# A fused attention and MLP block: the second LayerNorm's factors of twelve tiles stored a chunk ahead, the MLP's last block evacuated at once, three buffers of normalised rows in the front

## The chip, the cores and the metric

The kernel runs on one core of a Trainium2 chip. The metric is the device time of one execution in microseconds (us), the median of several. The core has five engines that work side by side, each through its own list of instructions in the order in which they were written: TensorE (PE, matrix products, transposes, with its weight loads shown as PEld), VectorE (DVE), ScalarE (ACT), GpSimd (POOL) and SyncE (SP), which here only issues DMAs. An engine waits at an instruction until what it needs has been produced by the others, and everything behind that instruction on the same engine waits with it.

## What is computed

The input x has 2048 rows of 448 values. The reference, cut to what matters:

```python
xn = _layernorm(x)
out = x + A(xn, wq, wk, wv, wo) + B(xn, w1, b1, w2, b2)

# A: 16 heads of 28, one shared key and value head
q = (x @ wq).reshape(B, S, H, Dh); k = x @ wk; v = x @ wv
p = softmax(einsum("bhqd,bkd->bhqk", q, k) * Dh ** -0.5)
o = einsum("bhqk,bkd->bhqd", p, v) @ wo

# B: pre-LayerNorm, 448 -> 1792 -> 448
y = _layernorm(x)
h = gelu(einsum("bsd,df->bsf", y, w1) + b1)
o = einsum("bsf,fd->bsd", h, w2) + b2
```

The MLP normalises rows that are normalised already. Their mean is zero, so the second LayerNorm is one factor for each row, worked out from the first one's variance and reciprocal deviation. The kernel multiplies the product with w1 by that factor.

## The kernel before

Products are taken to fp32 accuracy by splitting each operand into a high and a low part (names ending in h and l) and adding three products: high by low, high by high, low by high. The 2048 rows are 16 tiles of 128, in four chunks of four tiles (512 rows). Three stages follow each other on PE.

**Front: normalising and projecting, to about 64 us.** For each chunk c, `q_slot(c, i)` with i = 0 to 3 (L349) makes one quarter of the query, key and value columns: eleven matmuls on PE into a PSUM bank `qp`. The pieces around them are written slot by slot in the loop at L429. After slot (c, i) stand the evacuation of the slot before (`evac`, L357: ACT copies the high part to `qe`, DVE subtracts to get the low part, SP stores both to DRAM in `qd`; for i = 0 also the key `ks`, `kl` and the value `vt`, which PE turns in `v_slot`), then the parts of the next chunk's preparation, then w1's or w2's splitting, then further jobs from a table (`later`, L402). The preparation of a chunk (`norm_parts`, L258) has two parts for each tile k. *Centre* (`c`): ACT writes the normalised rows to a buffer `xn` (L271), DVE the last 64 columns again (L272, called the tail in what follows). *Turn* (`t`): four PE transposes into a PSUM buffer `m` (L280), ACT copies the high part `xh` (L281), DVE subtracts the low part `xl` (L282). There are three PSUM buffers `m`, in turn, and two buffers `xn`. The statistics are DVE's `bn` (L207, one per tile) and `bn_end` (L211 and the reciprocal chain of `rstd`, L189).

**The second LayerNorm's factors.** `norm_both` (L228) makes the factors of all 16 tiles in three steps, after slots (2,2), (2,3) and (3,0): products and first step of the reciprocal chain on DVE, the rest of the chain, then a PE transpose (L237), DVE's copy to `rows` (L239) and SP's store to `second` in DRAM (L240). `load_factors` (L248) reads 512 of them back, spread over all 128 partitions, into an `xn` buffer; it stands after slots (3,1) and (3,2) for the first two chunks of the MLP, which takes the chunks in the order 2, 3, 0, 1.

**MLP, to about 354 us.** There are 56 blocks, n = 14c + ft: a chunk by 128 of the 1792 hidden columns. Slot n runs `mlp1` of block n (L585: eleven first-layer matmuls into `ph`, for the blocks 1 to 3 into an `m` buffer; DVE multiplies by the factors at L592 into `hx`; ACT squares it into `hz` and adds the bias; *inner*, DVE L599; *middle*, tanh on ACT L602 and DVE L603; *ending*, ACT L609 copies `hh`, DVE L610 subtracts `hl`) and `mlp2` of block n − 3 (L614: twelve matmuls of 448 columns with `w2h`, `w2l` at L621, L624 and L627 into four PSUM banks `m2`). Middle and ending of a block are written one slot later, behind the next block's multiply (L592 to L594). w2 is split in the first chunk's slots (ACT L340, DVE L343); `w2h` and `w2l` take the storage that the front's buffers, `qe` among them, had before. With a chunk's last block DVE adds the four `m2` banks to the rows `a` (L631). In the last four blocks of chunk 3 (n = 52 to 55) a few jobs of the attention's start are written between matmuls: `first_shift` (DVE L533), `first_exp` (ACT L536), `first_back` (DVE L542), and one early score each.

**Attention and output, to the end.** Scores on PE (L681), exponents on ACT (L682), products with the values on PE (L870), then the output projection. Scores take the PSUM storage of `m2` once the MLP is over.

Of the kernel before, what the change touches and what calls it, by code (L numbers as in the profile page):

```python
# [40 lines left out]
def block_kernel(ctx, tc, x, wq, wk, wv, wo, w1, b1, w2, b2, out):  # L41
# [4 lines left out]
    def f(t):  # L46
        return t.bitcast(F32)
# [23 lines left out]
    lnq = wp.tile([P, NT], F32, name="lnq")  # L71
# [156 lines left out]
    def norm_both():  # L228
        dve.tensor_mul(lnq, lnp[:, :, 1], lnr)
        dve.tensor_mul(lnq, lnq, lnr)  # L230
        r = rstd(lnq, lnq, NT)
        next(r)
        yield
        next(r)
        yield
        turned = mtile([NT, P])
        pe.transpose(turned, lnq, ident)  # L237
        rows = wp.tile([NT, P], F32, name="rows")
        dve.tensor_copy(rows, turned)  # L239
        nc.sync.dma_start(second, rows)  # L240
        act.activation(warm, one, AF.Tanh)
        yield
# [5 lines left out]
    def load_factors(c):  # L248
        factors[c] = tmp.tile([P, CW], F32, name="xn", bufs=2)
        nc.sync.dma_start(factors[c], second[CT * c:CT * c + CT, :].rearrange("k p -> (k p)")[None, :].to_broadcast([P, CW]))  # L250
# [7 lines left out]
    def norm_parts(c, first=False, bank=mtile):  # L258
# [3 lines left out]
        xns = {}  # L262

        def center(k):
            t = CT * c + k
            if first:
                xn = f(wqp.tile([P, 2, CW], F32R, name="qe", bufs=5))[:, 0, :]
            else:
                xn = tmp.tile([P, 4 * P], F32, name="xn", bufs=2)
            scale, bias, src = lnr, lnb, xin[t]  # L270
            act.activation(xn[:, 0:D], src, AF.Identity, bias=bias[:, t:t + 1], scale=scale[:, t:t + 1])  # L271
            dve.tensor_scalar(xn[:, D:512], src[:, 384:448], scale[:, t:t + 1], bias[:, t:t + 1],  # L272
                              op0=ALU.mult, op1=ALU.add)
            xns[k] = xn

        def turn(k):
            sl = slice(k * P, (k + 1) * P)
            pt = bank([P, 4, P])
            for b in range(4):
                pe.transpose(pt[:, b, :], xns[k][:, b * P:(b + 1) * P], ident)  # L280
            act.activation(xh[:, :, sl], pt, AF.Copy)  # L281
            dve.tensor_sub(xl[:, :, sl], pt, f(xh[:, :, sl]))  # L282

        return center, turn

    def norm_first(bank):
        center, turn = norm_parts(0, True, bank)
# [117 lines left out]
    for c, at in ((2, ((0, 1), (0, 2), (0, 2), (0, 3))), (3, ((1, 0), (1, 1), (1, 2), (1, 3)))):  # L405
# [5 lines left out]
    g = norm_both()  # L411
    for c, k in ((2, 2), (2, 3), (3, 0)):
        later(c, k, lambda g=g: next(g))
# [15 lines left out]
    for c in range(NCH):  # L429
        if c + 1 < NCH:  # L430
            center, turn = norm_parts(c + 1)
        for i in range(4):
# [9 lines left out]
            for part, k in (("", "c0 c1", "t0 c2 t1 c3", "t2 t3") if c == 0 else  # L442
                            ("c0 c1", "t0 c2 t1 c3", "t2 t3", ""))[i].split() if c + 1 < NCH else ():
                (center if part == "c" else turn)(int(k))
# [5 lines left out]
            if (c, i) in ((3, 1), (3, 2)):  # L450
                load_factors(MLP_ORDER[i - 1])
# [133 lines left out]
    def mlp1(c, ft, before):  # L585
# [6 lines left out]
        dve.tensor_mul(hx, ph, factors[MLP_ORDER[c]])  # L592
        for job in before:
            job()  # L594
# [41 lines left out]
    def slot(n):  # L636
# [383 lines left out]
```

## Time and profile before

| | us |
|---|---|
| median of 3 runs | 905.06 (904.57 to 905.09) |
| the profiled execution | 903.79 |
| its span in the trace | 902.0 |
| PE busy in it | 886.1 (98%) |
| ACT busy | 703.6 (78%) |
| DVE busy | 488.4 (54%) |
| POOL busy | 68.6 (8%) |

The profiled execution is one of its own, so its time differs a little from the median, and what lies outside its span is 1.8 us. PE's mean granted clock is 0.995 of full speed. The page cuts the span into 40 slices of 22.55 us:

```profile
PE   9998999999999999999999999999999999999997
PEclk9998999999999999999999999999999999999999
```

Each digit is the busy share, or for PEclk the granted clock, in tenths. Both show 9 (90% or more) nearly throughout. The fourth slice (67.7 to 90.2 us) holds the start of the MLP; there both rows show an 8. The last holds the end of PE's work.

### The profile page before, as it was taken

How to read it: one execution, taken by the hardware profiler on the slowest of the kernel's cores; microseconds unless marked ns; L12 is line 12 of the kernel's file. 1: busy time of each engine (PE TensorE's matmuls, PEld its weight loads, DVE VectorE, ACT ScalarE, POOL GpSimd, SP SyncE). 2: the span in 40 equal slices, each digit the busy share in tenths (PEclk: the TensorE clock that was granted, in tenths of full speed). 3: DMA queues.
4: the chain of work that ended last, by engine and by line, in shares of the span. 5: the costliest groups of instructions: out<-in, count | busy, mean ns of one | idle time of the engine just before them, and what ended most of it. 6: DMA issues, size and time to landing. Idle time of an engine off the chain costs nothing.

```text
span 902.0 us, 13217 instructions
## 1 busy us (share of the span) xinstructions
PE 886.1 (98%) x4914; PEld 566.0 (63%) x4914; DVE 488.4 (54%) x975; ACT 703.6 (78%) x1334; POOL 68.6 (8%) x70
## 2 busy tenths in 40 slices
PE   9998999999999999999999999999999999999997
PEld 8776888888888886444444564444564444564445
DVE  6855676556556776654564544554544554544212
ACT  5765565555545456999999969999969999969992
POOL 4350000000000002031000000000000000000000
PEclk9998999999999999999999999999999999999999
DMA  9994133004002013031102211002211002211001
GB/s 290 323 285 138 42 114 125 10 20 162 6 1 77 6 42 115 9 78 43 22 21 57 70 41 43 18 25 55 70 41 43 22 22 55 71 41 41 3 1 44
DMA packets 36297, 60.69 MB, mean 67 GB/s; under 512 B 7782, under 2 KB 23348, under 8 KB 35204
## 3 DMA queue, kind: packets, MB, share of 16 engines
q1 hardware_dynamic: 34820, 59.22, 21.6%
q8 instruction: 40, 0.66, 0.3%
q10 hardware_dynamic: 1408, 0.57, 0.2%
q14 instruction: 29, 0.24, 0.1%
HBM read 39.89 MB, written 18.88 MB: 65 GB/s over the span
## 4 chain that ended last, share of the span: by engine, by line
PE 87%; ACT 5%; DVE 4%; DMA 3%; issue 1%; SPq 0%; ACTq 0%; DVEq 0%
PE m L681 26%; PE po L870 25%; PE ph L177 11%; PE m L627 5%; PE m L624 5%; PE m L621 4%; ACT p L682 2%; PE m L521 2%; PE m L757 1%; PE m L758 1%; PE m L759 1%; PE ph L180 1%; PE ph L182 1%; PE qp L177 1%; DMA second<-rows 1%
## 5 line engine op out<-in xcount | busy, mean ns | idle before, releaser
L682 ACT ACTIVATE p<-m 128x512 f32<-128x512 f32 x956 | 490.1, 758 | 30.2 <-PE m L681 29.7
L681 PE MATMUL m<-xh,ks 128*128 128x512 f32 x960 | 272.6, 410 | 0.6 <-DVE tt L528 0.3
L681 PEld LDWEIGHTS m<-xh,ks 128*128 128x128 f32 x960 | 174.3, 188 | 149.4 <-ACT p L682 76.3
L870 PE MATMUL po<-p,vs 128*32 128x512 f32 x2016 | 242.4, 598 | 0.0
L595 ACT ACTIVATE hz<-hx,b1s 128x512 f32<-128x512 f32 x56 | 40.6, 726 | 112.8 <-DVE hx L592 112.8
L870 PEld LDWEIGHTS po<-p,vs 128*32 128x32 f32 x2016 | 52.6, 109 | 115.8 <-issue 115.8
L528 DVE STREAM_TRANSPOSE tt<-m 128x512 f32<-128x512 f32 x60 | 43.0, 716 | 110.6 <-PE m L521 110.6
L621 PE MATMUL m<-w2h,hh 128*128 128x448 f32 x224 | 83.1, 371 | 5.1 <-ACT w2h L340 3.8
L624 PE MATMUL m<-w2l,hh 128*128 128x448 f32 x224 | 82.8, 370 | 0.4 <-DVE w2l L343 0.4
L627 PE MATMUL m<-w2h,hl 128*128 128x448 f32 x224 | 82.8, 370 | 0.2
L599 DVE SCALAR_TENSOR_TENSOR hz<-hz,hx 128x512 f32<-128x512 f32 x56 | 38.8, 692 | 53.7 <-ACT hx L596 53.7
L797 DVE COPY oc<-po 128x512 f32<-128x512 f32 x15 | 10.4, 692 | 103.2 <-PE po L870 103.2
L177 PE MATMUL ph<-xh,w1h 128*128 128x512 f32 x159 | 62.9, 396 | 0.1
L592 DVE TENSOR_TENSOR hx<-ph,xn 128x512 f32<-128x512 f32 x53 | 36.5, 690 | 48.5 <-PE ph L182 42.6
L177 PE MATMUL ph<-xh,w1l 128*128 128x512 f32 x159 | 62.3, 392 | 0.0
L177 PE MATMUL ph<-xl,w1h 128*128 128x512 f32 x159 | 62.3, 392 | 0.0
L812 POOL TENSOR_TENSOR otl<-oc,oth 128x512 fp32r<-128x512 f32 x15 | 23.9, 1591 | 470.4 <-DVE oth L810 274.1
L536 ACT ACTIVATE tt<-tt 128x512 f32<-128x512 f32 x60 | 50.0, 834 | 0.0
L621 PEld LDWEIGHTS m<-w2h,hh 128*128 128x128 f32 x224 | 42.6, 190 | 11.2 <-ACT w2h L340 4.3
L542 DVE STREAM_TRANSPOSE p<-tt 128x512 f32<-128x512 f32 x60 | 42.1, 702 | 12.0 <-ACT tt L536 12.0
L624 PEld LDWEIGHTS m<-w2l,hh 128*128 128x128 f32 x224 | 42.6, 190 | 5.4 <-DVE w2l L343 0.8
L627 PEld LDWEIGHTS m<-w2h,hl 128*128 128x128 f32 x224 | 42.6, 190 | 4.4 <-DVE hl L610 0.9
(174 smaller groups left out, 1033.1 us busy)
## 6 DMA issues: line engine op xcount, KB each, us to landing
xh<-qd SPq DMA_DIRECT2D x64, 224.0 KB
qd<-qe SPq DMA_DIRECT2D x24, 256.0 KB
a<-in_A_x_dram SPq DMA_DIRECT2D x20, 224.0 KB
ad<-a SPq DMA_DIRECT2D x16, 224.0 KB
a<-ad SPq DMA_DIRECT2D x16, 224.0 KB
raw<-in_B_w_dram SPq DMA_DIRECT2D x7, 448.0 KB
out_dram<-a SPq DMA_DIRECT2D x14, 224.0 KB
xd<-xh SPq DMA_DIRECT2D x2, 1024.0 KB
```

Source lines behind the costliest of these rows:

```text
L177: pe.matmul(ps, w, v, start=(n == 0), stop=False)
L528: dve.transpose(tts[u, j], pm)
L536: act.activation(tts[u, j], tts[u, j], AF.Exp, scale=SCALE)
L542: dve.transpose(p0s[u][:, j], tts.pop((u, j)))
L595: act.activation(hz, hx, AF.Square, bias=b1s[:, ft:ft + 1], scale=GELU[0] ** 0.5)
L599: dve.scalar_tensor_tensor(hz, hz, 1.0, hx, op0=ALU.add, op1=ALU.mult)
L621: pe.matmul(m2[k], hh[:, ts], w2h[:, ft, :], start=(ft == 0), stop=False)
L624: pe.matmul(m2[k], hh[:, ts], w2l[:, ft, :], start=False, stop=False)
L627: pe.matmul(m2[k], hl[:, ts], w2h[:, ft, :], start=False, stop=(ft == NF - 1))
L681: pe.matmul(s, ks[:, kt * P:(kt + 1) * P], qss[u][:, j, :], start=True, stop=True)
L682: act.activation(p, s, AF.Exp, scale=SCALE)
L870: pe.matmul(po[32 * j:32 * j + 32, :], vs[:, kt, :], ps.pop((u, kt, j)), start=(kt == 0), stop=(kt == NT - 1))
```

## The change

Three edits. **First**, `norm_both` becomes `norm_second(t0, n)`, which is called twice: for tiles 0 to 11 with its steps after slots (1,1), (1,2), (1,3), and for tiles 12 to 15 after (2,2), (2,3), (3,0). The load of the first MLP chunk's factors moves from after slot (3,1) to after (2,3). **Second**, `xn` has three buffers; the turn's low part becomes a part of its own (`l`), three centres stand in a chunk's first preparation slot instead of two, and the fourth comes one slot later between turns; the statistics of tile 10 move from slot (0,2) to (0,3). **Third**, in the MLP's last slot (n = 55), middle and ending of block 54 are written ahead of block 55's multiply, and inner, middle and ending of block 55 in the same slot, so that slot 56 has none left.

```diff
-    def norm_both():
-        dve.tensor_mul(lnq, lnp[:, :, 1], lnr)
-        dve.tensor_mul(lnq, lnq, lnr)
-        r = rstd(lnq, lnq, NT)
+    def norm_second(t0, n):
+        ts = slice(t0, t0 + n)
+        lnq = wp.tile([P, n], F32, name=f"lnq{n}")
+        dve.tensor_mul(lnq, lnp[:, ts, 1], lnr[:, ts])
+        dve.tensor_mul(lnq, lnq, lnr[:, ts])
+        r = rstd(lnq, lnq, n)
         next(r)
         yield
         next(r)
         yield
-        turned = mtile([NT, P])
+        turned = mtile([n, P])
         pe.transpose(turned, lnq, ident)
-        rows = wp.tile([NT, P], F32, name="rows")
+        rows = wqp.tile([n, P], F32, name=f"rows{n}")
         dve.tensor_copy(rows, turned)
-        nc.sync.dma_start(second, rows)
-        act.activation(warm, one, AF.Tanh)
+        nc.sync.dma_start(second[ts, :], rows)
+        if t0 + n == NT:
+            act.activation(warm, one, AF.Tanh)
         yield
...
-        factors[c] = tmp.tile([P, CW], F32, name="xn", bufs=2)
+        factors[c] = tmp.tile([P, CW], F32, name="xn", bufs=3)
...
-                xn = tmp.tile([P, 4 * P], F32, name="xn", bufs=2)
+                xn = tmp.tile([P, 4 * P], F32, name="xn", bufs=3)
...
             act.activation(xh[:, :, sl], pt, AF.Copy)
-            dve.tensor_sub(xl[:, :, sl], pt, f(xh[:, :, sl]))
-
-        return center, turn
+            pts[k] = pt
+
+        def low(k):
+            sl = slice(k * P, (k + 1) * P)
+            dve.tensor_sub(xl[:, :, sl], pts.pop(k), f(xh[:, :, sl]))
+
+        return center, turn, low
...
-    for c, at in ((2, ((0, 1), (0, 2), (0, 2), (0, 3))), (3, ((1, 0), (1, 1), (1, 2), (1, 3)))):
+    for c, at in ((2, ((0, 1), (0, 2), (0, 3), (0, 3))), (3, ((1, 0), (1, 1), (1, 2), (1, 3)))):
...
-    g = norm_both()
-    for c, k in ((2, 2), (2, 3), (3, 0)):
-        later(c, k, lambda g=g: next(g))
+    for t0, n, at in ((0, 3 * CT, ((1, 1), (1, 2), (1, 3))), (3 * CT, CT, ((2, 2), (2, 3), (3, 0)))):
+        g = norm_second(t0, n)
+        for c, k in at:
+            later(c, k, lambda g=g: next(g))
...
-            for part, k in (("", "c0 c1", "t0 c2 t1 c3", "t2 t3") if c == 0 else
-                            ("c0 c1", "t0 c2 t1 c3", "t2 t3", ""))[i].split() if c + 1 < NCH else ():
-                (center if part == "c" else turn)(int(k))
+            for part, k in (("", "c0 c1 c2", "t0 c3 l0 t1 l1", "t2 l2 t3 l3") if c == 0 else
+                            ("c0 c1 c2", "t0 c3 t1 l0 l1", "t2 l2 t3 l3", ""))[i].split() if c + 1 < NCH else ():
+                parts_of[part](int(k))
...
-            if (c, i) in ((3, 1), (3, 2)):
-                load_factors(MLP_ORDER[i - 1])
+            if (c, i) in ((2, 3), (3, 2)):
+                load_factors(MLP_ORDER[c - 2])
...
+        last = (c, ft) == mslots[-1]
+        if last:
+            for job in before:
+                job()
         hx = hrp.tile([P, CW], F32, name="hx", bufs=2)
         hz = hrp.tile([P, CW], F32, name="hz", bufs=2)
         dve.tensor_mul(hx, ph, factors[MLP_ORDER[c]])
-        for job in before:
-            job()
+        if not last:
+            for job in before:
+                job()
...
-            inner, *pending = yield from mlp1(*mslots[n], [middle])
-        else:
-            middle()
-        rest = ending()
-        inner()
-        rest()
+            if n == len(mslots) - 1:
+                inner, middle, ending = yield from mlp1(*mslots[n], [middle, lambda: ending()()])
+                inner()
+                middle()
+            else:
+                inner, *pending = yield from mlp1(*mslots[n], [middle])
+        if n < len(mslots):
+            rest = ending()
+            if n < len(mslots) - 1:
+                inner()
+            rest()
```

In the instruction lists the edits show at three places. The first is DVE in slots (1,1) to (1,2), from the evacuation of slot (1,0) on (`qe`, `kl`); line numbers are each kernel's own. Before:

```order
L367 TENSOR_TENSOR qe<-qp,qe 64x512
L369 TENSOR_TENSOR kl<-qp,ks 28x512
L282 TENSOR_TENSOR xl<-m,xh 128x4x128
L272 TENSOR_SCALAR xn<-a,lnr,lnb 128x64
L282 TENSOR_TENSOR xl<-m,xh 128x4x128
L272 TENSOR_SCALAR xn<-a,lnr,lnb 128x64
L207 BN_STATS st<-hh 128x6
L382 COPY vs<-m 128x128
L383 MEMSET vs 128x4
L367 TENSOR_TENSOR qe<-qp,qe 128x512
L282 TENSOR_TENSOR xl<-m,xh 128x4x128 x2
L207 BN_STATS st<-hl 128x6
```

After, in the same stretch and a little beyond:

```order
L379 TENSOR_TENSOR qe<-qp,qe 64x512
L381 TENSOR_TENSOR kl<-qp,ks 28x512
L274 TENSOR_SCALAR xn<-a,lnr,lnb 128x64
L288 TENSOR_TENSOR xl<-m,xh 128x4x128 x2
L206 BN_STATS st<-hh 128x6
L230 TENSOR_TENSOR lnq_552<-lnp,lnr 128x12
```

The products and the chain's first step go on for two rows; then come the copy and memset of `vs`, and after them on the same engine:

```order
L379 TENSOR_TENSOR qe<-qp,qe 128x512
L288 TENSOR_TENSOR xl<-m,xh 128x4x128 x2
L206 BN_STATS st<-hl 128x6
L194 RECIPROCAL rs_555<-rs_555 128x12
L195 SCALAR_TENSOR_TENSOR rs_555<-rs_555 128x12
L196 TENSOR_TENSOR rs_555<-rs_555 128x12
L197 SCALAR_TENSOR_TENSOR lnq_552<-rs_555 128x12
L379 TENSOR_TENSOR qe<-qp,qe 128x512
```

Tile 3's tail (L272, now L274) moved from between the subtracts to ahead of both, and the chain of twelve tiles' factors (`lnq_552`, L230 to L197) now stands between a statistics row and the next `qe` subtract. PE's turn of these factors stands between the last matmul of slot (1,3) and the first of slot (2,0), where nothing stood before; on PE after:

```order
L176 MATMUL qp<-xl,wah 128x512
L176 MATMUL qp<-xh,wal 128x512
L179 MATMUL qp<-xh,wah 128x512
L181 MATMUL qp<-xl,wah 128x512
L238 MATMUL m<-ident,lnq_552 12x128
L176 MATMUL qp<-xh,wah 128x512
L176 MATMUL qp<-xl,wah 128x512
L176 MATMUL qp<-xh,wal 128x512
```

What moved on PE is only the row L238, which needs DVE's `lnq`.

The second place is SP, from the evacuation of slot (2,0) to that of (3,0). Before (`raw` is w1 or w2 as loaded):

```order
L374 DMA qd_69<-qe 128x512
L374 DMA qd_70<-qe 128x512
L374 DMA qd_69<-qe 128x512
L374 DMA qd_70<-qe 128x512
L332 DMA raw<-in_B_w_dram 128x2x448
L374 DMA qd_69<-qe 128x512
L374 DMA qd_70<-qe 128x512
L332 DMA raw<-in_B_w_dram 128x2x448
L240 DMA second<-rows 16x128
L371 DMA ks<-kl 28x512 x2
L371 DMA ks<-ks 28x512
```

After:

```order
L386 DMA qd_69<-qe 128x512
L386 DMA qd_70<-qe 128x512
L386 DMA qd_69<-qe 128x512
L386 DMA qd_70<-qe 128x512
L252 DMA xn<-second 128x512
L344 DMA raw<-in_B_w_dram 128x2x448
L386 DMA qd_69<-qe 128x512
L386 DMA qd_70<-qe 128x512
L344 DMA raw<-in_B_w_dram 128x2x448
L241 DMA second<-rows_812 4x128
L383 DMA ks<-kl 28x512 x2
L383 DMA ks<-ks 28x512
```

The load `xn<-second` now stands ahead of w2's first raw load, and the store left in this place has four rows; the twelve-row store (`second<-rows_624`) stands in slot (1,3)'s place, before the last stores of chunk 1's queries.

The third place is DVE around the MLP's last block, from block 55's multiply (before) and block 54's middle (after) to the `m2` adds. Before:

```order
L592 TENSOR_TENSOR hx<-ph,xn 128x512
L603 SCALAR_TENSOR_TENSOR hx<-hz,hx 128x512
L599 SCALAR_TENSOR_TENSOR hz<-hz,hx 128x512
L610 SCALAR_TENSOR_TENSOR hl<-hx,hh 128x512
L533 TENSOR_TENSOR xl<-xl,mq 128x512
L542 STREAM_TRANSPOSE first<-xl 128x512
L697 TENSOR_TENSOR a<-a,b2b 128x448
L603 SCALAR_TENSOR_TENSOR hx<-hz,hx 128x512
L610 SCALAR_TENSOR_TENSOR hl<-hx,hh 128x512
L631 TENSOR_TENSOR a<-a,m_0_2617 128x448
```

After:

```order
L621 SCALAR_TENSOR_TENSOR hx<-hz,hx 128x512
L628 SCALAR_TENSOR_TENSOR hl<-hx,hh 128x512
L609 TENSOR_TENSOR hx<-ph,xn 128x512
L617 SCALAR_TENSOR_TENSOR hz<-hz,hx 128x512
L621 SCALAR_TENSOR_TENSOR hx<-hz,hx 128x512
L628 SCALAR_TENSOR_TENSOR hl<-hx,hh 128x512
L546 TENSOR_TENSOR xl<-xl,mq 128x512
L555 STREAM_TRANSPOSE first<-xl 128x512
L720 TENSOR_TENSOR a<-a,b2b 128x448
L649 TENSOR_TENSOR a<-a,m_0_2632 128x448
```

Block 55's multiply (L592, now L609) moved behind block 54's last two steps, and its own last two (L621, L628) moved from behind the bias add `a<-a,b2b` to ahead of the shift of `xl`.

More of the change, by code (lines that the diff above doesn't have):

```diff
@@ L70, in block_kernel @@
     lnr = wp.tile([P, NT], F32, name="lnr")
-    lnq = wp.tile([P, NT], F32, name="lnq")
     lnb = wp.tile([P, NT], F32, name="lnb")
@@ L261, in norm_parts @@
         xts[c] = xh, xl
-        xns = {}
+        xns, pts = {}, {}
         def center(k):
@@ L281, in turn @@
             act.activation(xh[:, :, sl], pt, AF.Copy)
-            dve.tensor_sub(xl[:, :, sl], pt, f(xh[:, :, sl]))
-        return center, turn
+            pts[k] = pt
[3 more added lines that the diff above has]
+        return center, turn, low
     def norm_first(bank):
-        center, turn = norm_parts(0, True, bank)
+        center, turn_high, turn_low = norm_parts(0, True, bank)
+        def turn(k):
+            turn_high(k)
+            turn_low(k)
         ends = [bn_end(0, 0, 2), bn_end(0, 2, 2)]
@@ L430, in block_kernel @@
         if c + 1 < NCH:
-            center, turn = norm_parts(c + 1)
+            parts_of = dict(zip("ctl", norm_parts(c + 1)))
         for i in range(4):
```

## The prediction

> **What bounds the kernel now.** I read the chain of waits first, since it names the engine on which a microsecond counts.
>
> ```profile
> PE 87%; ACT 5%; DVE 4%; DMA 3%; issue 1%; SPq 0%; ACTq 0%; DVEq 0%
> ```
>
> TensorE (PE) sets the end, so the change is worth what it does to PE's gaps and clock, not to anyone's busy time. Next the list of PE's waits, for gaps the change could touch:
>
> ```profile
> PE m L621 <- ACT w2h L340: 3.8, 1, 3.8
> PE m L621 <- ACT hh L609: 1.3, 1, 1.3
> ```
>
> The first is where the MLP starts, the second is its last block: the change works at both. Then the timeline at the MLP's start (start, duration, engine, operation, idle time before it):
>
> ```profile
> 60.80 1.25 SPq L240 DMA_DIRECT2D second<-rows  x1
> ...
> 66.29 0.39 PE L182 MATMUL ph<-xl,w1h 128*128 128x512 f32 x1
> ...
> 68.11 0.35 SPq L250 DMA_DIRECT2D xn<-second  x1
> ...
> 70.00 2.67 SPq L374 DMA_DIRECT2D qd<-qe  x4
> ...
> 71.55 0.69 DVE L592 TENSOR_TENSOR hx<-ph,xn 128x512 f32<-128x512 f32 x1 [5.95 <-DMA xn<-second]
> ...
> 73.84 0.40 PE L182 MATMUL m<-xl,w1h 128*128 128x512 f32 x1
> ...
> 77.08 0.95 ACT L340 ACTIVATE w2h<-raw 128x896 fp32r<-128x896 f32 x1
> ...
> 78.06 1.09 DVE L343 TENSOR_TENSOR w2l<-raw,w2h 128x896 fp32r<-128x896 f32 x1
> 78.08 0.74 PE L621 MATMUL m<-w2h,hh 128*128 128x448 f32 x1 [3.85 <-ACT w2h L340]
> ...
> 83.49 0.50 PE L177 MATMUL ph<-xh,w1h 128*128 128x512 f32 x1
> ```
>
> Block 0's product was ready at 66.68 (66.29 + 0.39), yet DVE multiplied it only at 71.55, held by the factors: stored at 60.80, loaded back at 68.11. PE ran out of first-layer work at 74.07 (73.84 and the 0.23 by which a matmul over 512 columns follows another, eleven of them in 39.56 − 36.95 below, with a small start) and stood until 78.08. The windows of 2 us (length, busy time of PE, PEld, DVE, ACT and POOL, then PE's granted clock) show a second bill:
>
> ```profile
> 76.00:78.00 2.00, 0.00 (x0) 0.00 (x0) 1.29 (x2) 2.00 (x4) 0.00 (x0) 0.72 0.13 40
> 78.00:80.00 2.00, 1.53 (x3) 1.03 (x4) 1.94 (x3) 0.76 (x3) 0.00 (x0) 0.50 0.00 0
> ...
> 82.00:84.00 2.00, 2.00 (x7) 1.79 (x6) 1.89 (x3) 1.21 (x2) 0.00 (x0) 0.57 0.01 3
> ```
>
> The clock fell to half at about 76.9 (0.72 is full for 0.9 of the two us) and came back at about 83.7 (0.57), so the first twelve second-layer matmuls ran until 83.49. What they take at full clock, and when a stopped PE loses it, the end of the program shows:
>
> ```profile
> 895.41 0.36 PE L758 MATMUL m<-wol,oth 128*128 128x448 f32 x1
> 895.61 0.37 PE L759 MATMUL m<-woh,otl 128*128 128x448 f32 x1
> ```
>
> ```profile
> 898.00:900.00 2.00, 0.00 (x0) 0.00 (x0) 0.00 (x0) 0.00 (x0) 0.00 (x0) 0.88 0.17 57
> ```
>
> A matmul over 448 columns follows the one before by 0.20; PE stops at 895.98 and the clock falls at about 899.5.
>
> **Part 1: factors a chunk ahead (gain).** SP's new row order puts the load of the first MLP chunk's factors ahead of the first w2 load, before the old 60.80. A store and its load back took 71.55 − 60.80 = 10.75 us; the new store's rows are ready at about 43 (Part 2), twice that ahead of block 0's product. So block 0 is multiplied when its product is there. From the multiply, w2h began 5.53 us later (71.55 to 77.08) and w2l ended 7.60 later (78.06 + 1.09); counted from 66.68 these are 72.21 and 74.28, and PE arrives at 74.07 and needs w2l a matmul later: the gap closes, and with it what slowed the clock. Twelve matmuls at full clock take 12 × 0.20 = 2.4, so 83.49 becomes 74.07 + 2.4 = 76.5. **Gain at most 7.0; I take 6.7**, lower end 6.4, since w2l is ready only just in time.
>
> **Part 2: what the front pays.** The second store's chain and a third centre per chunk go to DVE and ACT in slots (1,1) to (1,3), where DVE is full:
>
> ```profile
> 38.00:40.00 2.00, 2.00 (x10) 1.66 (x9) 2.00 (x5) 1.52 (x3) 1.58 (x3) 1.00 1.12 434
> ```
>
> ```profile
> 30.20 1.41 ACT L271 ACTIVATE xn<-a,lnb,lnr 128x448 f32<-128x448 f32 x2 [1.10 <-DVE lnb L217]
> ...
> 33.47 0.69 DVE L367 TENSOR_TENSOR qe<-qp,qe 64x512 fp32r<-64x512 f32 x1 [2.26 <-ACT vt L366]
> ...
> 35.52 0.30 DVE L272 TENSOR_SCALAR xn<-a,lnr,lnb 128x64 f32<-128x64 f32 x1
> 35.74 0.68 DVE L282 TENSOR_TENSOR xl<-m,xh 128x512 fp32r<-128x512 f32 x1
> ...
> 36.95 0.48 PE L177 MATMUL qp<-xh,wah 128*128 128x512 f32 x1
> ...
> 39.31 0.62 DVE L207 BATCH_NORM_STATS2 st<-hl 128x6 f32<-128x448 f32 x1
> ...
> 39.56 0.39 PE L177 MATMUL qp<-xh,wah 128*128 128x512 f32 x1
> ```
>
> - One more centre ahead of the evacuation costs ACT 1.41 / 2 = 0.70, and DVE's first qe subtract waits for vt: 33.47 becomes 34.17. Tile 3's tail (0.22 from its start to the next row's) now stands ahead of the subtracts of tiles 0 and 1, and PE's turns of tiles 2 and 3 need the PSUM buffers that those free: 0.70 + 0.22 puts q(1,3) at 36.95 + 0.92 = 37.87.
> - PE's turn of the twelve tiles' factors stands between q(1,3) and q(2,0). PE would be there at 37.87 + 39.56 − 36.95 = 40.5. DVE's list up to there is today's from 33.47 to 39.31 (5.84, with one tail less: 5.62), the statistics of 39.31 (0.62), and the factors' chain, new here. Its price stands in today's run at slot (2,3), beside GpSimd's split of w1; the last row is one of its steps elsewhere:
>
> ```profile
> 52.14 0.26 DVE L229 TENSOR_TENSOR lnq<-lnp,lnr 128x16 f32<-128x16 f32 x1
> ...
> 53.64 0.76 DVE L196 SCALAR_TENSOR_TENSOR rs<-rs 128x16 f32<-128x16 f32 x1
> ...
> 54.65 0.54 DVE L198 SCALAR_TENSOR_TENSOR lnq<-rs 128x16 f32<-128x16 f32 x1
> ```
>
> ```profile
> 52.71 1.66 POOL L327 TENSOR_TENSOR w1l<-raw,w1h 128x672 fp32r<-128x672 f32 x1 [0.34 <-POOL w1h L328]
> ```
>
> ```profile
> 42.62 0.16 DVE L196 SCALAR_TENSOR_TENSOR rs<-rs 128x4 f32<-128x4 f32 x1
> ```
>
> From 52.14 to 55.19 are 3.05, less one qe subtract of 0.69 among them 2.36; with both long steps at 0.16 it would be 1.38. So lnq is ready at 34.17 + 5.62 + 0.62 + 1.38 or 2.36 = 41.8 or 42.8: **PE stalls 1.3 to 2.3, and with some 0.3 for the turn itself q(2,0) begins at 42.1 to 43.1 instead of 39.56**, 2.5 to 3.5 late.
> - Chunk 3's preparation pays for the third centre as chunk 2's did, but by then its chain hangs on statistics that are late already: I add 0.5, half of 0.92 and a guess between 0 and that. The last four rows' job at (2,2) to (3,0) takes the places of today's sixteen rows': nothing.
>
> Together the front's end moves by 2.5 to 4.4; **I take 3.6**. No cover is left on DVE: its next row with idle time after 33.47 stands behind 41.56.
>
> **Part 3: last block.** Today:
>
> ```profile
> 343.60 0.68 DVE L592 TENSOR_TENSOR hx<-ph,xn 128x512 f32<-128x512 f32 x1
> ...
> 347.04 0.68 DVE L533 TENSOR_TENSOR xl<-xl,mq 128x512 f32<-128x512 f32 x1
> ...
> 349.06 0.58 DVE L697 TENSOR_TENSOR a<-a,b2b 128x448 f32<-128x448 f32 x1
> ...
> 350.28 0.63 ACT L609 ACTIVATE hh<-hx 128x512 fp32r<-128x512 f32 x1 [1.37 <-DVE hx L603]
> ...
> 352.19 2.47 DVE L631 TENSOR_TENSOR a<-a,m 128x448 f32<-128x448 f32 x4 [0.56 <-PE m L627]
> ...
> 354.72 1.66 PE L681 MATMUL m<-xh,ks 128*128 128x512 f32 x6
> ```
>
> After, block 54's middle and ending run first: DVE 343.60, ACT 344.3, DVE 345.0, one step of 0.63 to 0.69 behind the other, and block 55's multiply at 345.6 instead of 343.60. From there six such steps follow without a job between them (two on ACT, hz55, tanh, hx55): hh55 at about 349.9, 0.4 before 350.28, and hl55 until 351.2. But DVE waits for ACT in these steps with the first-exponent jobs queued behind them: the shift of 347.04 comes at 351.2. From the shift to the end of the bias add are 349.64 − 347.04 = 2.6, so the four m2 adds start at 353.8 instead of 352.19. The six scores at 354.72 wait for the last of those adds, whose PSUM they take: they begin at about 356.2 (354.66 + 1.6), and the 0.4 is lost under it. Later nothing wins it back, since ACT, with the attention's exponents, is full:
>
> ```profile
> 366.00:370.00 4.00, 4.00 (x29) 1.82 (x21) 1.96 (x4) 4.00 (x9) 0.00 (x0) 1.00 0.04 6
> ```
>
> **I take a loss of 1.4** (ends −0.4, if only hh55 counts, and 1.6).
>
> **Sum** against the profiled execution's 903.79 us (span 902.0): −6.7 + 3.6 + 1.4 = −1.7, so 902.1. The median shown, 905.06, is 1.27 above it; on that scale **903.4**. With the front at 2.5 or 4.4 it is 902.3 or 904.2. What a measurement can tell from no change is 0.2%, 1.81 us: the forecast lies at that border.
>
> **Rivals.**
> - *The last block's delay is absorbed.* ACT stands idle before its first attention exponent:
>
> ```profile
> 354.27 0.60 ACT L682 ACTIVATE p<-m 128x512 f32<-128x512 f32 x1 [2.39 <-PE m L681]
> ```
>
> So it might not matter when that begins. Then −0.4 instead of +1.4: **901.6**. Against it: PE is the engine that waits there, and it has 4.00 of 4.00 busy afterwards.
> - *The front stall doesn't bind*, because DVE's row order lets the chain finish while PE is busy: 0.92 for the centre and 0.3 for the turn remain, −6.7 + 1.2 + 1.4 = −4.1, **901.0**. Against it speaks the sum of the rows.
> - *The clock falls at a new stall* (40.5 to 42.8, or 354.2 to 356.2). It fell 2.8 us after PE stopped at 74.07 and 3.5 after 895.98; stalls of 1.3 to 2.3 are shorter than both. If it falls all the same, half pace for the 3.4 us that are half of 76.9 to 83.7 costs 1.7: **905.1**, and for all of it 906.8. The Trainium skill, page "TensorE: Matmul & The Clock Gate", Part 1 (The HAM clock gate), has a free-running window of about 3.4 us: after one idle window the clock is half, after one busy window full. By it a stall that fills most of one window could already suffice, and the sum would be this rival's 905.1; the trace agrees so far that 76.9 to 83.7 is twice 3.4.
> - *Slower: w2h waits for the last query stores.* It lies in the storage of the query buffers, so ACT's copy of 77.08 must wait until the four stores issued from 70.00 to 72.67 have landed, which takes at most 77.08 − 72.67 = 4.41 from the last issue. The four-row store keeps its place, 3.6 later, at 64.4. If it again needs 7.3 (60.80 to the load at 68.11), SP stands before the second factor load until 71.7, then issues that and the four stores by 74.8, and w2h may start as late as 79.2. PE is there at 77.7 and needs w2h one copy (0.95) before that, so from 76.7 on each microsecond is lost: up to 2.5, **905.9**; and with the clock falling again, as after 74.07, up to 3.0 more (twelve matmuls took 83.49 − 78.08 = 5.4 instead of 2.4), **908.9**. Against it: today the stores had landed some time before 77.08, since w2h stands there behind other ACT work.
>
> **How the numbers follow.** Forecast 903.4 with 0.50 (0.24 of it beyond −0.2%, 0.26 within); last block absorbed 0.13 (faster); front not binding 0.08 (faster); clock falls 0.16 (0.14 within, 0.02 slower); w2 wait 0.13 (0.02 within, 0.11 slower). Faster 0.45, same 0.42, slower 0.13. The range runs from 901.0, which takes in the absorbed block, to 906.9, the clock's dearer end and the w2 wait without the clock.
>
> **What would show it.** Part 1: the wait on w2h under 0.5, L592's first idle time no longer ended by the factors, the clock at 1.00 from 60 to 90. Part 2: a PE wait of 1.3 to 2.3 on the new turn (L238), and the matmul of 66.29 later by 2.5 to 4.4. Part 3: hh55 earlier by 0.4 and the scores behind the m2 adds later by 1.5, both against the start of that slot. The forecast is wrong if L238 shows no wait, if the w2h wait stays above 1, or if a window of half clock appears after 20 us.

## The result, and the profile after

The changed kernel takes 909.40 us (median of six runs, 908.37 to 910.58), the kernel before beside it 904.34: a ratio of 1.0057, with a 95% interval from 1.0044 to 1.0070. That is slower by 5.1 us, where 1.7 us faster was forecast, and it lies outside the range. The profiled execution took 908.37 us, its span is 906.3.

The waits of PE in the changed kernel (total, times, longest, in us) show first that neither of the two gaps of before was closed, and that three new ones came:

```profile
PE m L282 <- DVE xl L288: 2.6, 2, 1.5
PE m L639 <- ACT w2h L352: 1.7, 1, 1.7
PE m L704 <- DVE a L649: 1.6, 1, 1.6
PE m L639 <- ACT hh L627: 1.4, 1, 1.4
...
PE m L238 <- DVE lnq L197: 1.3, 1, 1.3
...
PE m L642 <- DVE w2l L355: 0.7, 1, 0.7
```

xl (L288), lnq (L238) and the m2 adds (L704) are new. The wait on w2h fell from 3.8 to 1.7, but did not go. The timeline at the MLP's start, in the order of the rows that the prediction read:

```profile
71.26 0.39 PE L181 MATMUL ph<-xl,w1h 128*128 128x512 f32 x1
...
71.69 0.69 DVE L609 TENSOR_TENSOR hx<-ph,xn 128x512 f32<-128x512 f32 x1 [1.24 <-PE ph L181]
...
73.76 2.27 SPq L386 DMA_DIRECT2D qd<-qe  x4
...
76.08 3.25 SPq L478 DMA_DIRECT2D km<-ks  x4
...
78.93 0.39 PE L181 MATMUL m<-xl,w1h 128*128 128x512 f32 x1
80.00 0.95 ACT L352 ACTIVATE w2h<-raw 128x896 fp32r<-128x896 f32 x1 [2.68 <-DMA km<-ks]
...
81.00 0.47 PE L639 MATMUL m<-w2h,hh 128*128 128x448 f32 x1 [1.68 <-ACT w2h L352]
...
85.94 0.48 PE L176 MATMUL ph<-xh,w1h 128*128 128x512 f32 x1
```

Block 0's product comes 4.97 us later than before (71.26 for 66.29). It is now multiplied as soon as it is there: the wait in front of L609 ends on PE and not on the factors. But ACT, idle for 2.68 us, may not begin w2h before a DMA has landed. PE stops again, and so the MLP's fifth block begins at 85.94 instead of 83.49. The granted clock (first number after the engines' busy times) is half in two places instead of one:

```profile
36.00:38.00 2.00, 0.53 (x5) 0.44 (x5) 1.94 (x5) 1.74 (x3) 0.60 (x1) 1.00 0.98 348
38.00:40.00 2.00, 2.00 (x9) 1.71 (x9) 1.93 (x5) 1.35 (x4) 1.70 (x2) 0.58 1.06 439
40.00:42.00 2.00, 2.00 (x7) 1.57 (x6) 1.92 (x5) 1.39 (x3) 0.48 (x1) 0.57 1.03 426
...
82.00:84.00 2.00, 1.87 (x6) 1.73 (x7) 1.27 (x3) 1.26 (x2) 0.00 (x0) 0.67 0.39 96
84.00:86.00 2.00, 2.00 (x7) 1.76 (x7) 1.68 (x3) 1.33 (x3) 0.00 (x0) 0.50 0.35 134
```

And the last block, DVE's shift, the m2 adds, and the scores behind them:

```profile
355.35 0.69 DVE L546 TENSOR_TENSOR xl<-xl,mq 128x512 f32<-128x512 f32 x1
...
357.87 2.20 DVE L649 TENSOR_TENSOR a<-a,m 128x448 f32<-128x448 f32 x4
...
360.13 1.66 PE L704 MATMUL m<-xh,ks 128*128 128x512 f32 x6 [1.62 <-DVE a L649]
```

To see where the time went, I put five points of PE and DVE beside each other, counted from each trace's first projection matmul of slot (0,0): the first matmul of block 0 (front's end), the first second-layer matmul, the first matmul of block 4, DVE's multiply of block 54, and PE's last matmul. All are read from the timelines, in us; "before, again" is a second trace of the kernel before.

| kernel | front's end | second layer | block 4 | multiply 54 | last matmul |
|---|---|---|---|---|---|
| before | 51.44 | 65.52 | 70.93 | 325.08 | 883.05 |
| before, again | 52.16 | 65.92 | 71.31 | 325.45 | 883.48 |
| changed | 56.38 | 68.45 | 73.39 | 329.17 | 888.50 |
| last block only | 52.16 | 65.65 | 71.04 | 325.42 | 884.74 |
| preparation only | 53.40 | 65.61 | 71.01 | 325.77 | 883.72 |
| factors only | 56.06 | 68.21 | 72.97 | 328.97 | 886.93 |
| layout only | 52.31 | 67.98 | 73.37 | 329.29 | 887.22 |
| w1 64 bytes lower | 51.51 | 65.00 | 69.86 | 325.75 | 883.68 |
| hh and w2 512 lower | 51.52 | 64.84 | 69.82 | 323.98 | 881.89 |
| changed, w2 split | 56.74 | 66.98 | 69.49 | 326.78 | 886.11 |
| early chain | 52.34 | 65.73 | 71.13 | 325.68 | 883.64 |
| early chain, w2 split | 52.35 | 62.42 | 65.09 | 320.69 | 878.65 |

The changed kernel against the first row: +4.94 at the front's end, −2.48 won back by block 4 (+2.46), +1.63 more by block 54 (+4.09), +1.36 more at the end (+5.45). The two traces of the kernel before differ by 0.72 at the front's end and 0.4 later; differences below that are not read from a single trace.

### The profile page after: what moved, and what is told of

Read it like the earlier page. It is cut to its first block, busy times and chain, and to the rows that moved or that the text cites. A ratio compares the mean times of both kernels' runs of the same rounds, so it can differ in the third digit from the quotient of the medians.

```text
span 906.3 us, 13226 instructions
## 1 busy us (share of the span) xinstructions
PE 888.6 (98%) x4915; PEld 566.3 (62%) x4915; DVE 491.9 (54%) x983; ACT 704.8 (78%) x1335; POOL 68.3 (8%) x70
## 4 chain that ended last, share of the span: by engine, by line
PE 88%; DVE 5%; ACT 4%; issue 1%; DMA 1%; SPq 0%; ACTq 0%; DVEq 0%
PE m L704 26%; PE po L893 25%; PE ph L176 12%; PE m L642 4%; PE m L645 4%; PE m L639 4%; PE qp L176 2%; ACT p L705 2%; PE m L534 2%; PE m L780 1%; PE m L781 1%; PE m L782 1%; PE ph L179 1%; PE ph L181 1%; DVE xl L288 0%
## 5 line engine op out<-in xcount | busy, mean ns | idle before, releaser
L704 PE MATMUL m<-xh,ks 128*128 128x512 f32 x960 | 272.7, 410 | 2.3 <-DVE a L649 1.6
L704 PEld LDWEIGHTS m<-xh,ks 128*128 128x128 f32 x960 | 174.3, 187 | 151.0 <-ACT p L705 76.3
L609 DVE TENSOR_TENSOR hx<-ph,xn 128x512 f32<-128x512 f32 x53 | 36.6, 690 | 45.0 <-PE ph L181 44.9
```

What stands on the lines that cost most here:

```text
L704: pe.matmul(s, ks[:, kt * P:(kt + 1) * P], qss[u][:, j, :], start=True, stop=True)
```

## The experiments

Every time ratio below is against the kernel before, run beside it, with its 95% interval.

**The kernel before, again.** No edit.

> The kernel before, unchanged, for its trace on this chip. If the longer spacing of the MLP's matmuls in the changed kernel (0.2330 us for 512 columns instead of 0.2308, 0.2036 for 448 instead of 0.2023) comes from the kernel's own layout, this run shows 0.231 and 0.202 again; if it comes from the chip or the moment, this run may show 0.233 and 0.204 too. Time within 0.2% of the runs of before beside it.

Measured: 1.0003 (0.9993 to 1.0013). Taken on average over the MLP from 100 to 320 us, consecutive matmuls of one kind stand 0.2307 us apart with 512 columns and 0.2026 with 448, as in the first trace (0.2306 and 0.2026); in the changed kernel 0.2327 and 0.2038. The longer spacing belongs to the kernel, not to the moment. All spacings below are this average.

**The last block only.** The third edit of the diff on the kernel before.

> Only the last block's edit. Theory (first-exponent jobs queued behind DVE's waits): the six scores behind the m2 adds come 1.3 us later against block 55's slot, and the time is 1.3 us longer (0.15%). Rival (absorbed by the attention): scores later, time equal or 0.4 shorter.

Measured: 1.0010 (1.0000 to 1.0020), and in the table +1.26 at the last matmul against the second trace of before, none of it before block 54. Its timeline has the wait of the changed kernel:

```profile
356.49 1.64 PE L691 MATMUL m<-xh,ks 128*128 128x512 f32 x6 [1.63 <-DVE a L636]
```

The scores wait 1.63 us for the m2 adds, and the attention does not take it up: the distance from the multiply of block 54 to the end is 559.32, against 557.97 before. The theory stands and the rival falls by the trace; the time alone, with an interval from 0 to 1.8 us, would leave both open.

**The preparation only.** The second edit on the kernel before: three buffers, three centres first, the low part apart.

> Only the third centre, the separate low part and the third buffer; factors stored and loaded as before. Theory (two stalls together took the clock in the changed kernel): PE waits about 1.5 us for xl in slot (1,2), the clock stays full from 30 to 60 us, the front ends 1.5 to 2 us later, the MLP's gap on the factors stays, and the time is 1.5 to 2 us longer. Rival (this stall alone takes the clock): a window of half clock near 38 us, the front 3 to 3.5 us later, the time 3 us longer.

Measured: 1.0015 (1.0004 to 1.0026), the medians 0.3 us apart. PE waits 1.54 us for xl, as expected, and the clock stays full behind that wait:

```profile
36.00:38.00 2.00, 0.46 (x5) 0.38 (x6) 1.94 (x4) 2.00 (x4) 0.20 (x1) 1.00 1.11 436
38.00:40.00 2.00, 2.00 (x13) 1.71 (x13) 1.92 (x6) 1.60 (x4) 1.92 (x2) 1.00 0.99 418
```

The front ends 1.2 to 2.0 us late, but block 4 begins where it began before (71.01). DVE's multiply of block 0 still waits for the factors, so the delay ran into the gap that is there anyhow:

```profile
72.04 0.69 DVE L602 TENSOR_TENSOR hx<-ph,xn 128x512 f32<-128x512 f32 x1 [4.16 <-DMA xn<-second]
```

The time leaves open how much comes through (0.4 to 2.4 us by the interval, 0.3 by the medians), and from block 4 on the trace has 0.2 to 0.7 us. My expectation, that the whole delay goes through to the end, is not borne out by the trace.

**The factors only.** The first edit on the kernel before, with two buffers and the old order of centres and turns.

> Only the split of the factors and the early load; two buffers and the old order of centres and turns. Theory: one stall of 1.3 to 2 us at the turn of the twelve tiles' factors, full clock there, the front ends 2 to 2.5 us later; the wait on w2h is ended by the last query stores and not by the factors, so that no more than 3 us are won at the MLP's start: time -1 to +0.5 us. Rival (the factors' chain alone costs what the changed kernel lost in front): front 4 to 5 us later, time 2 to 3 us longer.

Measured: 1.0051 (1.0039 to 1.0064), 4.6 us and so nearly the whole loss. The expectation of −1 to +0.5 us missed. The rival's front came true (3.9 to 4.6 us later), but its time of 2 to 3 us did not. The new turn waits much longer than in the changed kernel, and the clock falls behind it:

```profile
37.28 1.24 DVE L230 TENSOR_TENSOR lnq<-lnp,lnr 128x12 f32<-128x12 f32 x1
```

```profile
43.55 0.27 PE L238 MATMUL m<-ident,lnq 128*12 128x128 f32 x1 [3.65 <-DVE lnq L197]
```

```profile
44.00:46.00 2.00, 2.00 (x7) 1.54 (x6) 1.78 (x9) 0.15 (x1) 0.00 (x0) 0.50 0.87 230
```

A product of 12 columns took 1.24 us. Block 4 begins 1.7 to 2.0 us later than before, and block 54 is another 1.9 later (256.00 from block 4 to 54, against 254.15): the second of these has nothing to do with the front, and it is what both expectations lacked.

**The layout only.** The kernel before, with the same instructions; two tiles are taken in other places, which puts w1h and w1l 64 bytes and hh, hl, hx, w2h and w2l 512 bytes lower in each partition, as in the factors-only kernel (64 and 512 bytes are what lnq and rows take of a partition).

```diff
-    lnq = wp.tile([P, NT], F32, name="lnq")
...
     def norm_both():
+        lnq = wp.tile([P, NT], F32, name="lnq")
...
-        rows = wp.tile([NT, P], F32, name="rows")
+        rows = wqp.tile([NT, P], F32, name="rows")
```

> The kernel before, with the tile lnq taken behind w1's tiles and rows from another pool: the same instructions, while w1h lies 64 bytes and hh, hl and w2h lie 512 bytes lower in each partition, as in the factors-only kernel. Theory (where the operands lie sets the spacing of the MLP's matmuls): 0.232 to 0.233 us for 512 columns and 0.204 for 448 instead of 0.231 and 0.2025, time 1.5 us longer (0.17%). Rival (the spacing came from the stalls or the clock's earlier fall): 0.231 and 0.2025 again, time within 0.1%.

Measured: 1.0014 (1.0004 to 1.0024). The spacing is 0.2327 and 0.2038. From the first matmul of block 4 to the multiply of block 54 before and here:

```profile
337.64 0.68 DVE L592 TENSOR_TENSOR hx<-ph,xn 128x512 f32<-128x512 f32 x1
```

```profile
85.92 0.63 PE L176 MATMUL ph<-xh,w1h 128*128 128x512 f32 x1
...
341.84 0.68 DVE L592 TENSOR_TENSOR hx<-ph,xn 128x512 f32<-128x512 f32 x1
```

Before, 337.64 − 83.49 = 254.15; here 341.84 − 85.92 = 255.92, though no instruction moved. In the changed kernel it is 255.78. So 1.6 to 1.8 us of the loss come from where the tiles lie. (Block 4 was late in this trace, too, by 2 us: PE waited 5.3 for w2h in it. That is the profiled execution's own; the time ratio, 0.4 to 2.2 us, has room for the spacing only.)

Two kernels part the two shifts. **w1 64 bytes lower**: only lnq moves, behind w1l, so that w1h and w1l lie 64 bytes lower, and with them the four small tiles in front of them (lnb, b1t, b1s, b2b); all behind them stays. **hh and w2 512 lower**: only rows moves, so w1 stays.

```diff
     def norm_both():
+        lnq = wp.tile([P, NT], F32, name="lnq")
```

> The kernel before with only w1h and w1l 64 bytes lower in each partition (lnq behind them); all other operands where they were. If w1's place sets the spacing of the first-layer matmuls, 512 columns follow at 0.232 to 0.233 us and 448 columns stay at 0.2025; the stretch from the first multiply of block 4's matmuls to block 54's multiply is about 1 us longer than before's 254.15. If it doesn't, both stay as before.

Measured: 1.0019 (1.0008 to 1.0030), spacing 0.2328 and 0.2038, block 4 to 54 in 255.89.

```diff
-        rows = wp.tile([NT, P], F32, name="rows")
+        rows = wqp.tile([NT, P], F32, name="rows")
```

> The kernel before with w1h and w1l where they were and everything behind them (hh, hl, hx, w2h, w2l) 512 bytes lower. If the place of hh, hl and w2h sets the spacing of the second-layer matmuls, 448 columns follow at 0.2035 to 0.204 us and 512 columns stay at 0.231; the same stretch is about 0.7 us longer than 254.15. If it doesn't, both stay as before.

Measured: 0.9997 (0.9985 to 1.0008), spacing 0.2307 and 0.2026, block 4 to 54 in 254.16. The 64 bytes of w1 and its small neighbours are the cause; of these tiles PE reads w1h and w1l alone in the MLP, but no run moved w1 without the others. All five kernels here with w1 lower have the long spacing, and none of the others. The first of the two expectations was half right: with w1 moved, the second-layer matmuls slow down as well, though neither hh nor w2h moved, and the stretch grew by 1.7 instead of 1 us. Why is open.

**The changed kernel, w2 split.** w2h and w2l as seven tiles each in two pools, so that the first three pairs lie where wah, wal and pair lay, and none of them on the query buffers.

```diff
+    wah_p = ph1a.enter_context(tc.tile_pool(name="wah", bufs=1))
...
-    hp = ph1b.enter_context(tc.tile_pool(name="hp", bufs=3))
+    hp = [ph1b.enter_context(tc.tile_pool(name=f"hp{i}", bufs=1)) for i in range(2)]
...
-    w2h = hp.tile([P, NF, D], F32R, name="w2h", bufs=1)
-    w2l = hp.tile([P, NF, D], F32R, name="w2l", bufs=1)
+    w2h, w2l = [], []
+    for s in range(NF // 2):
+        w2h.append(hp[s > 2].tile([P, 2, D], F32R, name=f"w2h{s}"))
+        w2l.append(hp[s > 2].tile([P, 2, D], F32R, name=f"w2l{s}"))
```

> The changed kernel, with w2h and w2l as seven tiles each in two pools, so that the first three pairs lie where wah, wal and pair lay and nothing of them where the query buffers lay. Theory (w2h waited for the last query stores, which land behind a full DMA queue): no wait on w2h at the first second-layer matmul, full clock from 60 to 90 us, that block's end 4.3 us earlier against the changed kernel: 0.5 to 1.5 us slower than before instead of 5.1. Rival (w2h waited for something else, such as its own chain from the first multiply): wait and clock as in the changed kernel, 5 us slower than before.

Measured: 1.0029 (1.0019 to 1.0039), some 2.5 us better than the changed kernel by the ratios, but still 2.6 slower than before, where 0.5 to 1.5 were expected. The wait on w2h is gone from the list and the clock at the MLP's start is full; block 4 begins 3.9 us earlier than in the changed kernel (69.49 for 73.39). So it was the query buffers' storage, that is, the stores out of it, that w2h waited for.

The completions of the DMAs, which the traces keep too, agree. In the four traces in which ACT stood idle just before the first w2h copy (changed, factors only, layout only, early chain), it begins 0.18 to 0.26 us after the last query store has landed (79.82 and 80.00 in the changed kernel); here it begins 3.3 us ahead of that landing. The name that the row gives for what ended the wait, km<-ks, is that of the copies issued right behind those stores; the first of them lands within 0.3 us of the last store.

Not all of the 3.9 us stays: until block 54 it falls to 2.4, since PE now waits 1.3 for an earlier multiply (L611), with ph's one bank. The front is the changed kernel's front, yet here the clock held through 36 to 40 and fell later, behind a longer wait for lnq (2.90):

```profile
36.00:38.00 2.00, 0.47 (x6) 0.39 (x6) 1.94 (x4) 2.00 (x4) 0.29 (x1) 1.00 0.96 305
38.00:40.00 2.00, 2.00 (x14) 1.67 (x13) 1.93 (x5) 1.19 (x3) 1.92 (x2) 1.00 1.08 438
44.00:46.00 2.00, 1.61 (x5) 1.34 (x6) 2.00 (x5) 0.00 (x0) 0.22 (x1) 0.60 0.81 225
```

**The early chain.** The kernel before, with its one chain of sixteen tiles after slots (2,0), (2,0) and (2,1), where DVE had no work from 44 to 46 us, and the first factor load after (2,3).

```diff
-    for c, k in ((2, 2), (2, 3), (3, 0)):
+    for c, k in ((2, 0), (2, 0), (2, 1)):
         later(c, k, lambda g=g: next(g))
...
-            if (c, i) in ((3, 1), (3, 2)):
-                load_factors(MLP_ORDER[i - 1])
+            if (c, i) in ((2, 3), (3, 2)):
+                load_factors(MLP_ORDER[c - 2])
```

> The kernel before, with one chain of all sixteen tiles as before but its steps after slots (2,0), (2,0) and (2,1), where DVE had 2 us without work, and the first factor load after (2,3). Theory: the front ends at most 0.5 us later; block 0 is multiplied when its product is there, and yet w2h starts only about 0.5 to 1 us earlier than before, when the last query stores have landed: time 0 to 2 us shorter. Rival (the factors were all that PE waited for): the gap closes, time 6 us shorter.

Measured: 0.9990 (0.9979 to 1.0002). The chain costs next to nothing at this place, and DVE's rows show why: GpSimd has no work there, and each of these steps takes 0.17 or 0.18 us:

```profile
44.09 0.17 DVE L229 TENSOR_TENSOR lnq<-lnp,lnr 128x16 f32<-128x16 f32 x1
...
45.55 0.18 DVE L196 SCALAR_TENSOR_TENSOR rs<-rs 128x16 f32<-128x16 f32 x1
...
45.98 0.18 DVE L198 SCALAR_TENSOR_TENSOR lnq<-rs 128x16 f32<-128x16 f32 x1
```

Block 0 is multiplied when its product is there, almost 4 us earlier than before, and yet w2h begins no earlier:

```profile
67.78 0.69 DVE L592 TENSOR_TENSOR hx<-ph,xn 128x512 f32<-128x512 f32 x1 [1.20 <-PE ph L182]
...
77.45 0.95 ACT L340 ACTIVATE w2h<-raw 128x896 fp32r<-128x896 f32 x1 [4.05 <-DMA km<-ks]
```

ACT sits idle 4.05 us. The gain that the whole change was about was closed to it from the start: behind the factors stood a second wait, almost as late.

**The early chain, w2 split.** Both edits on the kernel before.

> Both: the early chain and w2 in tiles that don't lie on the query buffers. Theory: neither factors nor stores hold anything, no wait of PE over 0.5 us between 60 and 90 us and full clock there, time 5.5 to 6.5 us shorter than before (0.65%). Rival (a further wait takes their place): under 3 us shorter.

Measured: 0.9951 (0.9936 to 0.9966), the best of all: 899.65 us, against 904.04 before. PE goes over to the second layer without a break, where the kernel before stood for four microseconds:

```profile
75.25 0.39 PE L183 MATMUL m<-xl,w1h 128*128 128x512 f32 x1
75.48 0.37 PE L623 MATMUL m<-w2h,hh 128*128 128x448 f32 x1
```

Block 4 begins 5.8 to 6.2 us earlier (65.09). At the end 4.4 to 4.8 are left: PE then waits 1.3 for the multiply of block 4, behind DVE's split of the second w2 pair. The expected 5.5 to 6.5 was reached at block 4 and not at the end.

**The last block with the jobs ahead.** The last block's edit, with the shift, exponent and transpose of the first scores one block earlier each.

```diff
-    firsts = {(NCH - 1, 10 + j): {13: f"s{j}", 16: f"x{j}", 20: f"b{j}"} for j in range(4)}
+    firsts = {(NCH - 1, 9 + j): {13: f"s{j}", 16: f"x{j}", 20: f"b{j}"} for j in range(4)}
```

> The last block's edit alone, with the first-exponent jobs one block earlier each (blocks 51 to 54 of the MLP instead of 52 to 55), so that none stands behind the last block's waits. Theory (those jobs behind DVE's waits cost the 1.3 us of the last-block-only kernel): no wait of the scores on the m2 adds beyond 0.5 us, the time 1.2 to 1.7 us shorter than the last-block-only kernel and 0 to 0.5 shorter than before. Rival (the m2 adds are late for another reason): the wait on them stays at 1.6, the time 1 us longer than before.

Measured: 1.0003 (0.9992 to 1.0014). The wait on the m2 adds is gone, and from the multiply of block 54 to the end are 557.70 us, 0.3 less than before: the forecast's 0.4 exists once nothing is queued behind it. But the jobs now hold up earlier blocks, where PE waits for the multiply, and block 4 to 54 takes 255.70 instead of 254.15:

```profile
PE ph L177 <- DVE hx L596: 1.0, 2, 0.6
```

The theory of the wait stands. The gain is given back: against the last-block-only kernel the time is some 0.6 us shorter by the ratios, not 1.2 to 1.7.

**All three**: the early chain, w2 split, and the last block with the jobs ahead.

> The early chain, w2 in tiles off the query buffers, and the last block's edit with the jobs one block earlier. Theory (the parts add up): 0 to 0.5 us shorter than the early chain with w2 in tiles, so 4.4 to 5 us shorter than before. Rival (the last block's edit gives nothing where it is not held up either): equal to the early chain with w2 in tiles.

Measured: 0.9965 (0.9951 to 0.9978), 901.15 us: not better than without the last block's edit (0.9951; the intervals overlap). PE's waits for multiplies are 2.4 us in three places instead of 1.3 in one, and its last matmul comes 1.0 later against the first (879.64 for 878.65). The parts do not add up here, and the last block's edit is better left out.

## Why the prediction was wrong, point by point

**Part 1, the gain of 6.7, failed.** The step was "block 0 is multiplied when its product is there", and from there w2h 5.53 us later, "the gap closes, and with it what slowed the clock". The first half came true (L609 waits for PE only). The second counted ACT's chain alone. w2h also has to wait until the last query stores have left the storage that it takes over. Before, ACT was busy up to 77.08, so this wait left no idle time in its row and no line in the list of waits; but the last of these stores landed at 76.83, 0.25 us ahead of w2h. The early chain shows the wait bare (4.05 us, landing at 77.19, w2h at 77.45), and the split of w2 takes it away. In the changed kernel the front's delay moved the stores back as well, and 2.48 instead of 6.7 came back. Even the 2.48 is no part of the forecast gain: the preparation alone, with the factors as late as before, wins back 1.88 of its 1.96 us in the same gap (against the first row of the table), and the early chain, which has the factors early and no late front, wins nothing by block 4.

This was the rival "w2h waits for the last query stores", to which I gave 0.13, with a price of 905.9, or 908.9 with the clock falling again; the range ended at 906.9, short of that price. The clock did fall (82 to 86 us). What spoke against the rival, that the stores "had landed some time before 77.08", was too easily said: it was 0.25 us. The rival's place was right and its reason partly wrong: SP did not stand before the second factor load, whose landing of the four rows I blamed. It issued stores almost without a break until 76.03, and the DMA engines were full: their share in the windows from 62 to 70 us was 1.00 to 1.25, from 70 to 76 us 0.77 to 0.90. I should have read the last stores' landing from the DMA's own rows, since it was the one term that decided between −7 and nothing.

**Part 2, the front, was mis-sized: 4.94 instead of 3.6** (4.2 against the second trace of before). The places were right, the prices were not. Slot (1,3) began 1.53 late instead of 0.92 (38.48 for 36.95): the centres of chunk 2 themselves began 0.72 late, and PE waited 1.54 for xl. Of the 0.72, 0.31 stand at the qe subtract behind the statistics row of tile 10 (28.00 for 27.69), which now comes a slot later, an edit that I had counted as nothing; 0.42 come from a small DVE step (L191) that took 0.59 instead of 0.17 beside a GpSimd subtraction.

From there to slot (2,0) it took 44.11 − 38.48 = 5.63 instead of the forecast's 4.2 to 5.2. The wait for lnq in it was 1.32, inside the forecast, but only because the clock had fallen and PE came late to it. What set slot (2,0) was lnq, ready at 43.94 instead of 41.8 to 42.8: DVE's list began at 34.85 instead of 34.17, and the steps of the chain took 2.80 together instead of 1.38 to 2.36. So slot (2,0) began 4.55 late instead of 2.5 to 3.5; chunk 3's preparation added 0.4, as forecast (0.5). That the clock could fall at a new stall was a rival of its own, with 0.16. It fell, but this first fall cost nothing by itself: where the clock held (changed kernel, w2 split), PE waited 2.90 for the same lnq instead of 1.32.

The mechanism behind the long steps of the chain is one that I had only priced from rows. In the changed kernel:

```profile
38.38 0.66 DVE L230 TENSOR_TENSOR lnq<-lnp,lnr 128x12 f32<-128x12 f32 x1
...
42.73 0.45 DVE L195 SCALAR_TENSOR_TENSOR rs<-rs 128x12 f32<-128x12 f32 x1
```

```profile
37.40 1.62 POOL L339 TENSOR_TENSOR w1l<-raw,w1h 128x672 fp32r<-128x672 f32 x1 [7.85 <-DMA raw<-in_B_w_dram]
...
41.52 1.63 POOL L339 TENSOR_TENSOR w1l<-pair,w1h 128x672 fp32r<-128x672 f32 x1 [1.74 <-issue]
```

The product ends at 39.04, GpSimd's subtraction at 39.02; the chain's step ends at 43.18, GpSimd at 43.15. Both DVE steps end as GpSimd's instruction ends; in the early chain, where GpSimd is idle, they take 0.17 and 0.18. The Trainium skill's page "SBUF — State Buffer", section "Who interferes with whom", says that a DVE instruction with both inputs in SBUF contends with a GpSimd instruction that reads SBUF, and that the pair of ports that the two engines share is an exclusive lock. The trace agrees to 0.03 us. The chain put into slots (1,1) to (1,3) stood beside w1's splitting, and at (2,0) it did not.

**Part 3, the last block, was right**: 1.36 lost for a forecast of 1.4, with the wait where it was expected; the gain at hh55, 0.4 in the forecast, is 0.28 against block 54's multiply. That the attention might absorb it (0.13) fell with the last-block-only kernel.

**A term was missing: 1.63 us from the place of w1.** The diff takes lnq out from in front of w1h, which moves w1 by 64 bytes. The forecast looked at what each tile waits for, never at where it lies. Nothing in the trace of before could have shown this price; it is the one part of the miss that a closer reading would not have found.

The four together: 4.94 − 2.48 + 1.63 + 1.36 = 5.45 us at PE's last matmul, and 5.1 in the time; the forecast had −6.7 + 3.6 + 1.4, and no fourth term.

## What to carry to other kernels

Before a wait is priced as gone, ask of the instruction behind it what else it waits for, and read when that was ready: a storage that changes owner has waits which an earlier, later-ending wait hides completely. A small DVE step on SBUF data can last until GpSimd's instruction beside it ends (0.45 to 1.24 us here instead of 0.17), so a chain of them belongs where GpSimd is idle. And a delay is free only while a gap behind it is there to take it up: the preparation's 1.2 to 2 us cost at most 0.26% alone, but with w2 split, where that gap is closed, the changed kernel's front ends 4.39 us later than the early chain's and block 4 begins 4.40 later.

## What the runs showed of the hardware that had not been expected

w1h and w1l, with four small tiles in front of them, 64 bytes lower in each partition, and no instruction changed, made consecutive matmuls of the MLP stand 0.2328 us apart instead of 0.2307 (512 columns) and 0.2038 instead of 0.2026 (448), over 254 us; 0.19% of the time (0.08 to 0.30). Weight loads and matmuls kept their durations within a few nanoseconds, and the second-layer matmuls, whose operands had not moved, slowed as well. Which property of the address does it stays open: only two places were tried.

The clock falls or holds behind the same wait. Behind some 1.54 us of waiting for xl, with PE busy for 0.46 to 0.53 us of the two from 36 to 38, it fell in the changed kernel (0.58 from 38 to 40) and held in preparation only and in the changed kernel with w2 split (1.00).

The Trainium skill's page "TensorE: Matmul & The Clock Gate", Part 1 (The HAM clock gate), speaks of a free-running window of about 3.4 us. These traces agree: between the start of the kernel and the end of PE's work, each stretch at half clock lasts 3.41 us or twice that, so the edges of such windows can be counted back from any change of the clock. In the changed kernel the wait (35.93 to 37.48) lies whole in the window from 34.9 to 38.32, at whose end the clock falls. In the two others an edge cuts it: at 37.75 the wait from 36.34 to 37.88, at 37.56 the one from 36.26 to 37.79. PE, transposes included, is busy 1.87 us of the window in the first, 2.01 and 2.12 in the others. So here the clock fell with PE busy for over half of a window, where the Trainium skill's page, as the prediction gives it, has one idle window. No run here moved the edges on purpose, so what share of a window suffices stays open.
